# One SBUF pool for each weight tile and each weight pair, and last-stage pools laid on the ones that fall free first

## The chip, the cores and the metric

The kernel runs on one core of a Trainium2 chip. The metric is the device time of one execution in microseconds (us); the median of three executions is compared. A core has TensorE (PE; its weight loads are PEld), VectorE (DVE), ScalarE (ACT), GpSimd (POOL) and SyncE (SP), which here issues every transfer (DMA). Each engine works through its own queue strictly in order: an instruction that waits holds everything behind it on that engine.

## The reference, cut to what matters

Three blocks follow each other on 4 sequences of 576 tokens with 512 features: a linear attention, a mixer with a low-rank token part, and a second mixer. All in float32.

```python
def _moe_ref(x, U, V, w_ch1, w_ch2):            # w_ch1 512 x 2048, w_ch2 2048 x 512
    h = x.transpose(0, 2, 1) @ U @ V
    u = x + h.transpose(0, 2, 1)
    return u + np.maximum(u @ w_ch1, 0.0) @ w_ch2
def _moe2_ref(x, w_tok1, w_tok2, w_ch1, w_ch2): # w_ch1 512 x 1536, w_ch2 1536 x 512
    h = np.maximum(x.transpose(0, 2, 1) @ w_tok1, 0.0) @ w_tok2
    u = x + h.transpose(0, 2, 1)
    return u + np.maximum(u @ w_ch1, 0.0) @ w_ch2
```

## The kernel before, in words

Matmuls run on pairs of float32r tiles, a rounded high part and the rest, so each product is three matmuls (high-high, high-low, low-high). `split` makes such a pair: a copy on one engine, a subtraction on another. Weights arrive as 64-bit numbers. `load64` brings a block of 128x512 of them (512 KB) into a buffer `raw` by a transfer on SP, makes `w` and `r` from it by two ACT instructions (L140, L141), and puts them together by two DVE instructions (L143, L146). The second of these reads `raw` for the last time, and the buffer may then be filled again.

There are three stages. Stage A is the attention with part of the first mixer's channel work. Stage B takes each batch b in two halves of 288 tokens: `channel` runs the remaining 11 blocks of the first mixer's channel weights (tiles `wh`, `wl` of block f; blocks 0 to 6 in `wrB`). For each block TensorE computes `hp`, ACT makes `hhb` of it and DVE `hlb` (`relu_split`), and TensorE adds block f's part to `yb` one block later. After both halves `tokmix2` does the second mixer's token part: transposes `x2p`, their splits `x2h` and `x2l`, products `gp`, `gh` and `gl`, products `m2p`, an addition to `x2` (L607) and a store to DRAM (`u2D`).

Stage C, the last one, is the second mixer's channel part, over five chunks of tokens (464 wide, the last 448). The 12 blocks of weights are taken as six pairs. `pair_weights(p)` needs four loads: `raw_c{p}_0` and `_1` for the first-layer tiles `sh`, `sl` (seven combinations, four of them built in a scratch tile `st` on DVE and split by ACT and POOL), and `_2` and `_3` for the second-layer tiles `vh`, `vl`. For each chunk, `token_mats` builds seven combinations `th`, `tl` of the tokens `uc`; then `first(p)` forms products of 42 matmuls in PSUM tiles `xc`, `yc`, `zc`, `vc`, and `second(p)` adds 24 matmuls to the output. The weights of the six pairs are made once, while chunk 0 runs, and kept.

`raw` in stage C has two buffers. SBUF is filled from two sides. Each tile pool gets an address range when it is opened; a pool opened after others were closed is laid over their ranges, and a tile of it waits until the tiles below it have been used for the last time. The order on each engine is not written by hand: the framework's scheduler chooses it when it builds the program, from when it thinks that buffers fall free.

Of the kernel before, what the change touches and what calls it, by code (L numbers as in the profile page):

```python
# [8 lines left out]
F32 = mybir.dt.float32  # L9
F32R = mybir.dt.float32r  # L10
# [9 lines left out]
P = 128  # L20
# [5 lines left out]
C = 512  # L26
NPAIR = H // 2
NC = C // P
# [3 lines left out]
NF2 = 12  # L32
NA = 5
NR = NF2 - NA
EPS = 1e-06
CHUNKS = (464, 464, 464, 464, 448)
HM = 232
# [51 lines left out]
def body(ctx, tc, kq, vd, w_phi, U, V, wm1, wt1, wt2, wm2, out):  # L89
# [36 lines left out]
    wring = AB.enter_context(tc.tile_pool(name="wring", bufs=NA))  # L126
# [24 lines left out]
    def load_half(src, i, name, k, hi, lo):  # L151
        sl = slice(k * C, (k + 1) * C)
        w = load64(src[i][:, sl], P, C, f"{name}_{k}")
        split(w, hi[:, sl], lo[:, sl], WHI[name[0]][k], WLO[name[0]][k])

    def w_tiles(pool, name, slot=""):
        return [pool.tile([P, 2 * C], F32R, tag=f"{t}{slot}", name=f"{t}_{name}") for t in ("wh", "wl")]

    def load_w(pool, src, i, name, slot=""):
        hi, lo = w_tiles(pool, name, slot)  # L160
        for k in range(2):
            load_half(src, i, name, k, hi, lo)
        return hi, lo
# [374 lines left out]

    BX = ExitStack()
    with tc.using_default_side("right"):  # L540
        wrB = BX.enter_context(tc.tile_pool(name="wrB", bufs=1, reuse_waits="tile"))
        extra.append(BX.enter_context(tc.tile_pool(name="rawx", bufs=RAWX, reuse_waits="tile")))
        bc = BX.enter_context(tc.tile_pool(name="bc", bufs=1, reuse_waits="tile"))
        b2 = BX.enter_context(tc.tile_pool(name="b2", bufs=2, reuse_waits="tile"))
# [3 lines left out]
    psg = PB.enter_context(tc.tile_pool(name="psg", bufs=1, space=PSUM, reuse_waits="tile"))  # L548

    nB = NF1 - NA  # L550
    wB = [load_w(wrB, wm1, NA + f, f"b{f}", f) if f < NR else load_w(wring, wm1, NA + f, f"b{f}") for f in range(nB)]

    def channel(ws, uh, ul, res, o, nm, dst=None, pool=mlp):
        n = uh.shape[2]
# [65 lines left out]
    for t in range(NT):  # L620
        w = load64(wt1[:, t], P, 256, f"t1_{t}")
# [3 lines left out]
    for j in range(2):  # L625
        for k in range(2):
            sl = slice(k * N, (k + 1) * N)
            w = load64(wt2[:, j, sl], P, N, f"t2_{j}_{k}")
            split(w, T2H[:, j, sl], T2L[:, j, sl], "v", "v")

    for b in range(B):
        x2 = b2.tile([P, NC, S], F32, tag="x2", name=f"x2_{b}", bufs=1)
        for ch in range(2):
            nm = f"b{b}_{ch}"
            i = 2 * b + ch
            _, uh, ul = load_u(uD[i], nm) if i else u0
# [7 lines left out]
    PB.close()  # L644
    extra.clear()
    with tc.using_default_side("right"):
        wc = ctx.enter_context(tc.tile_pool(name="wc", bufs=1, reuse_waits="tile"))
    stc = ctx.enter_context(tc.tile_pool(name="stc", bufs=RAWB, reuse_waits="tile"))
    pc = ctx.enter_context(tc.tile_pool(name="pc", bufs=1, reuse_waits="tile"))
    psc = ctx.enter_context(tc.tile_pool(name="psc", bufs=1, space=PSUM, reuse_waits="tile"))  # L650

    def pair_weights(p):
        nm = f"c{p}"
        wa, wb = [load64(wm2[2 * p + i][:, :C], P, C, f"{nm}_{i}", stage=stc, wbufs=3) for i in range(2)]
        sh, sl = [wc.tile([P, 7, 256], F32R, tag=f"{t}{p}", name=f"{t}{p}") for t in ("sh", "sl")]
        split(wa.rearrange("p (a k) -> p a k", a=2), sh[:, 0:2], sl[:, 0:2], "a", "v")
        split(wb[:, 256:], sh[:, 2], sl[:, 2], "a", "v")

        def comb(i, a, b, op):
            t = stc.tile([P, 256], F32, tag="st", name=f"st{p}_{i}")  # L660
            nc.vector.tensor_tensor(out=t, in0=a, in1=b, op=op)
            split(t, sh[:, i], sl[:, i], "a", "p")
            return t

        s1 = comb(3, wb[:, :256], wb[:, 256:], ALU.add)
        s2 = comb(4, s1, wa[:, :256], ALU.subtract)
        comb(6, wa[:, 256:], s2, ALU.subtract)
        comb(5, wa[:, :256], wb[:, :256], ALU.subtract)
        vh, vl = [wc.tile([P, 2, C], F32R, tag=f"{t}{p}", name=f"{t}{p}") for t in ("vh", "vl")]
        for i in range(2):  # L670
            w = load64(wm2[2 * p + i][:, C:], P, C, f"{nm}_{2 + i}", stage=stc, wbufs=3)
            split(w, vh[:, i], vl[:, i], "a", "pv"[i])
        return sh, sl, vh, vl
# [3 lines left out]
    def token_mats(u, h, nm):  # L677
        b11, b12, b21, b22 = u[:, 0:2, :h], u[:, 0:2, h:], u[:, 2:4, :h], u[:, 2:4, h:]
        m = {}

        def put(i, src):
            th, tl = [pc.tile([P, 2, HM], F32R, tag=f"{t}{i}", name=f"{t}{i}{nm}")[:, :, :h] for t in ("th", "tl")]
            split(src, th, tl, "a", "v")
            m[i] = th, tl

        def comb(o, a, b):
            nc.vector.tensor_tensor(out=o, in0=a, in1=b, op=ALU.subtract)

        put(0, b11)
        t1 = pc.tile([P, 2, HM], F32, tag="tt", name=f"tt{nm}")[:, :, :h]  # L690
        comb(t1, b12, b11)
        put(2, b22)
        comb(b11, b22, t1)
        put(4, b11)
        put(3, t1)
        comb(b12, b22, b12)
        put(5, b12)
        put(1, b21)
        comb(b21, b21, b11)
        put(6, b21)  # L700
        return m

    def channel7(sl_, nm):
        n = sl_.stop - sl_.start
        h = n // 2
        u = pc.tile([P, NC, 2 * HM], F32, tag="u", name=f"u{nm}")[:, :, :n]
        nc.sync.dma_start(u, u2D[:, :, sl_])
        m = token_mats(u, h, nm)
        res = []
        for c in range(NC):  # L710
            res.append(pc.tile([P, 2 * HM], F32, tag="res", name=f"res{nm}_{c}", bufs=4)[:, :n])
            nc.sync.dma_start(res[c], u2D[:, c, sl_])
        yp = [psy.tile([P, 512], F32, tag=f"y{c}", name=f"y{nm}_{c}") for c in range(NC)]

        def product(o, w, wi, ti, start):
            wh, wl = w[0][:, wi], w[1][:, wi]
            th, tl = m[ti]
            for k in range(2):
                ks = slice(k * P, (k + 1) * P)
                g = [(wh[:, ks], th[:, k]), (wh[:, ks], tl[:, k]), (wl[:, ks], th[:, k])]  # L720
                for i, (l, r) in enumerate(g):
                    mm(o, l, r, start and k == 0 and i == 0, k == 1 and i == 2)

        def first(p):
            w = wC[p]
            pm = f"{nm}_{p}"
            X, Y, Z, V = [psc.tile([P, 512], F32, tag=t, name=f"{t}{pm}")[:, :h] for t in ("x", "y", "z", "v")]
            product(X, w, 0, 0, True)
            e = pc.tile([P, HM], F32, tag="e", name=f"e{pm}")[:, :h]
            cp("a", e, X)  # L730
            product(Y, w, 4, 4, True)
            product(Z, w, 3, 3, True)
            product(V, w, 5, 5, True)
            u2 = pc.tile([P, HM], F32, tag="u2", name=f"u2{pm}")[:, :h]
            nc.vector.tensor_add(u2, Y, e)
            hb = pc.tile([P, 2 * HM], F32, tag="hb", name=f"hb{pm}")[:, :n]
            nc.vector.tensor_add(hb[:, h:], V, u2)
            nc.vector.tensor_add(hb[:, h:], Z, hb[:, h:])
            product(X, w, 1, 1, False)
            product(V, w, 2, 6, False)  # L740
            product(Z, w, 6, 2, False)
            nc.vector.tensor_add(hb[:, :h], V, u2)
            ha = pc.tile([P, HM], F32, tag="ha", name=f"ha{pm}")[:, :h]
            nc.vector.tensor_add(ha, Z, u2)
            out2 = []
            for i in range(2):
                s = (2 * p + i) % 3
                out2.append([pc.tile([P, 2 * HM], F32R, tag=f"{t}{s}", name=f"{t}{pm}_{i}")[:, :n] for t in ("hh", "hl")])
            (ah, al), (bh, bl) = out2
            relu_split(X, ah[:, :h], al[:, :h])  # L750
            relu_split(ha, ah[:, h:], al[:, h:])
            relu_split(hb, bh, bl)
            return out2

        def second(p, hs):
            vh, vl = wC[p][2:]
            for i, (hh, hl) in enumerate(hs):
                for c in range(NC):
                    cs = slice(c * P, (c + 1) * P)
                    g = [(vh[:, i, cs], hh), (vh[:, i, cs], hl), (vl[:, i, cs], hh)]  # L760
                    for k, (l, r) in enumerate(g):
                        mm(yp[c][:, :n], l, r, p == 0 and i == 0 and k == 0, p == NF2 // 2 - 1 and i == 1 and k == 2)

        prev = None
        for p in range(NF2 // 2):
            hs = first(p)
            if prev is not None:
                second(*prev)
            prev = (p, hs)
        second(*prev)  # L770
        for c in range(NC):
            nc.vector.tensor_add(res[c], yp[c][:, :n], res[c])
            nc.sync.dma_start(out[:, c, sl_], res[c])

    t = 0
# [64 lines left out]
```

## Time and profile before

| what | value |
|---|---|
| median of three runs | 1117.73 us (1114.35 to 1120.58) |
| profiled execution: its own time | 1113.12 us |
| profiled execution: its span | 1111.3 us |
| TensorE matmuls | 1045.1 us busy, 94% |
| TensorE weight loads | 978.6 us, 88% |
| VectorE | 667.2 us, 60% |
| ScalarE | 458.5 us, 41% |
| GpSimd | 236.5 us, 21% |

Span is from the first to the last instruction; the own time also holds what lies around it. The shares are averages over stages of quite different kinds, so they say little about one place. Stage C begins at about 776 us of the span.

### The profile page before, as it was taken

The numbers are of one execution on the slowest core, as the hardware profiler recorded it, in microseconds if no ns is written. First come the engines' busy times: TensorE is split into PE (matmuls) and PEld (weight loads), VectorE is DVE, ScalarE is ACT, GpSimd is POOL, SyncE is SP. The second block draws the span as 40 slices with busy tenths as digits, with TensorE's granted clock in tenths as the row PEclk, the third lists the DMA queues.
The fourth block names the chain that finished last, engine by engine and source line by source line (L and its number), as shares of the span: only waits on it lengthen the run. The fifth ranks groups of instructions, "written<-read, shape, count | busy, mean of one in ns | idle before, by whom it ended". The sixth has DMA issues, their size and how long they took to land.

```text
span 1111.3 us, 18092 instructions
## 1 busy us (share of the span) xinstructions
PE 1045.1 (94%) x7068; PEld 978.6 (88%) x7068; DVE 667.2 (60%) x1221; ACT 458.5 (41%) x1079; POOL 236.5 (21%) x192
## 2 busy tenths in 40 slices
PE   9888999899899898999999999997687999999998
PEld 6777899799789698999999999996676899999998
DVE  7888997987995797523223214217788636363533
ACT  6776756665754675221111111115566313121211
POOL 3326655555643244000000000000233100000000
PEclk9998999999999798999999999999879999999999
DMA  6542322312211685102002101205433303020110
GB/s 208 173 133 62 117 70 73 97 56 79 81 55 38 216 284 169 42 22 86 22 9 80 42 1 44 81 1 172 136 123 133 103 1 104 1 94 9 37 33 34
DMA packets 62501, 92.18 MB, mean 83 GB/s; under 512 B 14672, under 2 KB 49232, under 8 KB 62416
## 3 DMA queue, kind: packets, MB, share of 16 engines
q1 hardware_dynamic: 62416, 91.03, 25.8%
q8 instruction: 55, 0.90, 0.3%
q14 instruction: 30, 0.25, 0.1%
HBM read 71.99 MB, written 18.95 MB: 82 GB/s over the span
## 4 chain that ended last, share of the span: by engine, by line
PE 69%; DVE 14%; DMA 7%; ACT 6%; issue 3%; POOL 1%; SPq 0%; DVEq 0%; ACTq 0%; POOLq 0%
PE yc L107 12%; PE hp_b L107 12%; PE yb L107 12%; PE hp_a L107 4%; PE yp L107 4%; PE pp L107 3%; PE vc L107 3%; PE xc L107 3%; PE zc L107 3%; PE kvp L107 3%; DMA raw_c<-in_wm_dram 3%; PE gp L107 2%; PE nm L107 2%; PE m2p L107 2%; PE dT L356 2%
## 5 line engine op out<-in xcount | busy, mean ns | idle before, releaser
L182 DVE SCALAR_TENSOR_TENSOR hlb<-hp_b,hhb 128x288 fp32r<-128x288 f32 x88 | 40.1, 456 | 185.2 <-ACT hhb L181 185.2
L181 ACT ACTIVATE hhb<-hp_b 128x288 fp32r<-128x288 f32 x88 | 36.1, 410 | 228.5 <-PE hp_b L107 225.8
L107 PE MATMUL hp_b<-uhb,wh_b 128*128 128x288 f32 x352 | 105.2, 300 | 3.4 <-DVE xT L493 3.4
L107 PE MATMUL hp_b<-ulb,wh_b 128*128 128x288 f32 x352 | 105.1, 299 | 0.0
L107 PE MATMUL hp_b<-uhb,wl_b 128*128 128x288 f32 x352 | 105.0, 299 | 0.0
L100 POOL TENSOR_TENSOR sl<-st,sh 128x256 fp32r<-128x256 f32 x24 | 22.6, 956 | 380.1 <-ACT sh L95 379.9
L107 PE MATMUL yb<-hlb,wh_b 128*128 128x288 f32 x352 | 97.3, 296 | 0.2
L107 PE MATMUL yb<-hhb,wl_b 128*128 128x288 f32 x352 | 97.1, 295 | 0.0
L107 PE MATMUL yc<-hlc,vh 128*128 128x464 f32 (+1 forms) x240 | 90.5, 377 | 0.0
L107 PE MATMUL yc<-hhc,vl 128*128 128x464 f32 (+1 forms) x240 | 90.4, 377 | 0.0
L107 PE MATMUL yc<-hhc,vh 128*128 128x464 f32 (+1 forms) x240 | 84.6, 382 | 2.4 <-ACT hhc L181 2.4
L100 POOL TENSOR_TENSOR qel<-qe,qeh 128x640 fp32r<-128x640 f32 (+1 forms) x48 | 71.7, 1505 | 26.2 <-ACT qeh L95 11.2
L107 PEld LDWEIGHTS hp_b<-uhb,wh_b 128*128 128x128 f32 x352 | 67.1, 191 | 4.9 <-DVE xT L493 3.7
L107 PE MATMUL yb<-hhb,wh_b 128*128 128x288 f32 x352 | 68.0, 296 | 0.0
L107 PEld LDWEIGHTS hp_b<-ulb,wh_b 128*128 128x128 f32 x352 | 67.4, 192 | 0.1
L107 PEld LDWEIGHTS hp_b<-uhb,wl_b 128*128 128x128 f32 x352 | 67.2, 191 | 0.0
L107 PEld LDWEIGHTS yb<-hlb,wh_b 128*128 128x128 f32 x352 | 66.1, 188 | 0.6 <-DVE hlb L182 0.6
L107 PEld LDWEIGHTS yb<-hhb,wl_b 128*128 128x128 f32 x352 | 66.3, 188 | 0.0
L100 POOL TENSOR_TENSOR kel<-ke,keh 128x512 fp32r<-128x512 f32 x36 | 48.6, 1362 | 62.5 <-ACT keh L95 61.0
L288 DVE TENSOR_REDUCE km<-pp 128x4 f32<-128x512 f32 x80 | 54.5, 682 | 12.3 <-PE pp L107 12.0
L100 DVE TENSOR_TENSOR kd<-pp,km 128x512 f32<-128x512 f32 x80 | 54.4, 681 | 0.7
L107 PEld LDWEIGHTS yb<-hhb,wh_b 128*128 128x128 f32 x352 | 53.9, 188 | 0.1
(249 smaller groups left out, 3209.1 us busy)
## 6 DMA issues: line engine op xcount, KB each, us to landing
raw_c<-in_wm_dram SPq DMA_DIRECT2D x24, 512.0 KB, 3.8
raw_b<-in_wm_dram SPq DMA_DIRECT2D x22, 512.0 KB, 4.6
kq<-in_kq_dram SPq DMA_DIRECT2D x80, 128.0 KB, 2.2
raw_a<-in_wm_dram SPq DMA_DIRECT2D x10, 512.0 KB, 4.4
rec<-rD SPq DMA_DIRECT2D x32, 144.0 KB, 2.9
uD<-xT SPq DMA_DIRECT2D x8, 576.0 KB, 3.5
sD<-xT SPq DMA_DIRECT2D x8, 576.0 KB, 5.4
x<-sD SPq DMA_DIRECT2D x8, 576.0 KB, 5.1
```

Of the source, the lines that this page charges most:

```text
L100: return ENG[e].tensor_tensor(out=o, in0=a, in1=b, op=ALU.subtract)
L107: nc.tensor.matmul(o, l, r, start=start, stop=stop, skip_group_check=True)
L181: nc.scalar.activation(hh, hp, AF.Relu)
L182: nc.vector.scalar_tensor_tensor(out=hl, in0=hp, scalar=0.0, in1=f32(hh), op0=ALU.max, op1=ALU.subtract)
L288: nc.vector.tensor_reduce(out=m, in_=pv, op=ALU.max, axis=AX.X, apply_absolute_value=True)
L356: nc.tensor.transpose(tp[:, o : o + r], ds["q", g, t][:r, j, :], ident[:r, :r])
```

## The change

The pool `wrB`, which held the tiles of seven blocks, becomes seven pools of one block each. The pool `wc`, which held the tiles of six pairs, becomes six pools of one pair each, all opened at the same point. Their tiles are made up front instead of inside `pair_weights`. The two scratch tiles `st` move from the small pool `stc` into the pool of pair 0, so that `stc` is now as large as the pool `stage` that it lies on. The tiles of `token_mats` and the tokens `uc` get a pool `pt` of their own. By the sizes, pair 0 with the scratch lies exactly on blocks 0 to 2, pair 1 on blocks 3 to 5, pair 2 on the rest of block 5, block 6 and the extra raw buffers. No arithmetic is added or taken away; the number of instructions on each compute engine and of bytes moved stays.

```diff
-        wrB = BX.enter_context(tc.tile_pool(name="wrB", bufs=1, reuse_waits="tile"))
+        wrB = [BX.enter_context(tc.tile_pool(name=f"wrB{f}", bufs=1, reuse_waits="tile")) for f in range(NR)]
...
-        wc = ctx.enter_context(tc.tile_pool(name="wc", bufs=1, reuse_waits="tile"))
+        wc = [ctx.enter_context(tc.tile_pool(name=f"wc{p}", bufs=1, reuse_waits="tile")) for p in range(NF2 // 2)]
     stc = ctx.enter_context(tc.tile_pool(name="stc", bufs=RAWB, reuse_waits="tile"))
+    pt = ctx.enter_context(tc.tile_pool(name="pt", bufs=1, reuse_waits="tile"))
     pc = ctx.enter_context(tc.tile_pool(name="pc", bufs=1, reuse_waits="tile"))
...
+    wcs = {}
+    for p in range(NF2 // 2):
+        w = wc[p]
+        wcs[p] = [w.tile([P, 7, 256], F32R, tag=f"{t}{p}", name=f"{t}{p}") for t in ("sh", "sl")]
+        wcs[p] += [w.tile([P, 2, C], F32R, tag=f"{t}{p}", name=f"{t}{p}") for t in ("vh", "vl")]
+        if p == 0:
+            sts = [w.tile([P, 256], F32, tag=f"st{i}", name=f"st{i}") for i in range(2)]
...
-        sh, sl = [wc.tile([P, 7, 256], F32R, tag=f"{t}{p}", name=f"{t}{p}") for t in ("sh", "sl")]
+        sh, sl, vh, vl = wcs[p]
...
-            t = stc.tile([P, 256], F32, tag="st", name=f"st{p}_{i}")
+            t = sts[i % 2]
...
-        u = pc.tile([P, NC, 2 * HM], F32, tag="u", name=f"u{nm}")[:, :, :n]
+        u = pt.tile([P, NC, 2 * HM], F32, tag="u", name=f"u{nm}")[:, :, :n]
```

The built program stands in the same order as before up to batch 0 of stage B, where five raw loads of stage C now go out on SP and three of them are turned into `w`. On TensorE the order is the same until the token part of the last batch (b3). The first place is the ACT queue in the second half of the last batch (names `hhb3_1_f`: batch 3, half 1, block f). Before, nothing stands between the blocks:

```order
L181 ACTIVATE hhb3_1_6_8865<-hp_b3_1_6_8852 128x288
L181 ACTIVATE hhb3_1_7_8894<-hp_b3_1_7_8881 128x288
L181 ACTIVATE hhb3_1_8_8923<-hp_b3_1_8_8910 128x288
L181 ACTIVATE hhb3_1_9_8952<-hp_b3_1_9_8939 128x288
L181 ACTIVATE hhb3_1_10_8981<-hp_b3_1_10_8968 128x288
L95 CAST x2h3_0_9020<-x2p3_0_9015 128x512
L95 CAST x2h3_1_9035<-x2p3_1_9030 128x512
L140 ACTIVATE w_c0_0_9185<-raw_c0_0_9183 128x512
```

With the change the same queue there reads so (`sh1` belongs to pair 1, `w_c1_2` to its third load):

```order
L181 ACTIVATE hhb3_1_6_8883<-hp_b3_1_6_8870 128x288
L140 ACTIVATE w_c1_1_9313<-raw_c1_1_9311 128x512
L141 ACTIVATE r_c1_1_9314<-raw_c1_1_9311 128x512
L95 CAST sh1_9231<-w_c1_0_9305 128x512
L140 ACTIVATE w_c1_2_9337<-raw_c1_2_9335 128x512
L141 ACTIVATE r_c1_2_9338<-raw_c1_2_9335 128x512
L181 ACTIVATE hhb3_1_7_8912<-hp_b3_1_7_8899 128x288
L95 CAST sh1_9231<-w_c1_1_9313 128x256
L95 CAST sh1_9231<-st1_9230 128x256
L95 CAST sh1_9231<-st0_9229 128x256
L181 ACTIVATE hhb3_1_8_8941<-hp_b3_1_8_8928 128x288
```

Weight work of pairs 0 to 2, which stood behind `x2h3_1`, now stands among the blocks from `hhb3_1_3` on. The second place follows at once, the ACT queue where the token part of batch 3 begins, with the change:

```order
L181 ACTIVATE hhb3_1_10_8999<-hp_b3_1_10_8986 128x288
L95 CAST sh2_9235<-w_c2_0_9357 128x512
L140 ACTIVATE w_c2_1_9365<-raw_c2_1_9363 128x512
L141 ACTIVATE r_c2_1_9366<-raw_c2_1_9363 128x512
L95 CAST x2h3_0_9038<-x2p3_0_9033 128x512
L140 ACTIVATE w_c2_2_9389<-raw_c2_2_9387 128x512
L141 ACTIVATE r_c2_2_9390<-raw_c2_2_9387 128x512
L95 CAST x2h3_1_9053<-x2p3_1_9048 128x512
```

Before, `x2h3_0` followed `hhb3_1_10` directly; now three instructions of pair 2 stand ahead of it and two ahead of `x2h3_1`. The third place is SP's queue around the stores of batch 3. Before, the order was this:

```order
L135 DMA raw_c1_0_9243<-in_wm2_dram 128x512
L707 DMA uc1_10138<-u2D_76 128x4x464
L608 DMA u2D_76<-x2_3_8344 512x1x288 x2
L135 DMA raw_c1_1_9251<-in_wm2_dram 128x512
L135 DMA raw_c1_2_9283<-in_wm2_dram 128x512
```

With the change it is this:

```order
L715 DMA uc1_10158<-u2D_76 128x4x464
L135 DMA raw_c3_2_9439<-in_wm2_dram 128x512
L608 DMA u2D_76<-x2_3_8362 512x1x288
L135 DMA raw_c3_3_9449<-in_wm2_dram 128x512
L608 DMA u2D_76<-x2_3_8362 512x1x288
L135 DMA raw_c4_0_9459<-in_wm2_dram 128x512
```

Ahead of the stores stand now 15 of the 24 weight loads in place of 5.

## Rows read from the trace of the kernel before

**Rows 1.** Page, busy tenths of TensorE in 40 equal slices of the span.

```profile
PE   9888999899899898999999999997687999999998
```

**Rows 2.** Stretches: length, busy us (instructions) by engine, TensorE's granted clock, DMA share, GB/s.

```profile
core 0: us, PE busy (x) PEld busy (x) DVE busy (x) ACT busy (x) POOL busy (x), PEclk, DMA share, GB/s
...
752.00:776.00 24.00, 19.32 (x109) 16.46 (x108) 18.88 (x37) 13.59 (x26) 1.42 (x2) 0.93 0.52 168
776.00:800.00 24.00, 17.04 (x94) 15.00 (x93) 17.82 (x34) 11.76 (x25) 7.48 (x7) 0.86 0.46 154
800.00:820.00 20.00, 15.17 (x65) 13.83 (x66) 16.04 (x29) 11.71 (x25) 5.53 (x6) 0.66 0.36 117
820.00:840.00 20.00, 15.08 (x90) 13.23 (x88) 15.12 (x29) 11.89 (x25) 4.49 (x5) 0.91 0.44 147
840.00:860.00 20.00, 15.07 (x85) 13.08 (x86) 17.50 (x35) 13.12 (x30) 7.73 (x6) 0.94 0.40 132
860.00:876.00 16.00, 15.25 (x105) 14.18 (x105) 12.52 (x24) 7.93 (x17) 4.01 (x4) 0.97 0.10 26
...
931.95:990.41 58.46, 58.46 (x398) 55.17 (x397) 28.23 (x63) 13.70 (x31) 0.00 (x0) 1.00 0.15 50
```

**Rows 3.** Timelines of ACT, DVE, TensorE: start, duration, instruction [idle before <-releaser].

```profile
752.57 0.59 ACT L95 CAST x2h<-x2p 128x512 fp32r<-128x512 f32 x1 [1.61 <-PE x2p L585]
...
766.10 1.27 DVE L182 SCALAR_TENSOR_TENSOR gl<-gp,gh 128x512 fp32r<-128x512 f32 x2
...
776.36 0.27 PE L107 MATMUL xc<-th0c,sh 128*128 128x232 f32 x1
...
780.93 0.56 PE L107 MATMUL xc<-th0c,sl 128*128 128x232 f32 x1 [3.97 <-DVE sl L100]
...
1107.29 0.37 PE L107 MATMUL yc<-hhc,vl 128*128 128x448 f32 x1
```

**Rows 4.** Chain that ended last, from 812 us: start, us, what.

```profile
812.78 3.78 DMA raw_c<-in_wm_dram
816.60 0.04 issue
816.65 0.67 ACT w_c L140
817.32 0.57 ACT r_c L141
...
819.21 0.61 DVE w_c L146
```

**Rows 5.** Timeline of SP's transfers, 690 to 880 us.

```profile
694.92 1.09 SPq L135 DMA_DIRECT2D raw_c<-in_wm_dram  x2
...
772.61 4.99 SPq L608 DMA_DIRECT2D u2D<-x  x2
785.61 70.96 SPq L135 DMA_DIRECT2D raw_c<-in_wm_dram  x19
```

**Rows 6.** Tile raw_c, transfers from issue to landing.

```profile
DMA to landing us min/median/max: 3.4/3.8/6.8
```

**Rows 7.** Timelines of TensorE, ACT and DVE in the last half-batch of stage B.

```profile
729.61 0.30 PE L107 MATMUL hp_b<-uhb,wh_b 128*128 128x288 f32 x1
...
747.37 0.41 ACT L181 ACTIVATE hhb<-hp_b 128x288 fp32r<-128x288 f32 x1 [2.77 <-PE hp_b L107]
...
747.81 0.46 DVE L182 SCALAR_TENSOR_TENSOR hlb<-hp_b,hhb 128x288 fp32r<-128x288 f32 x1 [2.73 <-ACT hhb L181]
```

**Rows 8.** Groups by shape, 776 to 876 us: busy us, mean ns, idle before.

```profile
L143 DVE SCALAR_TENSOR_TENSOR w_c<-w_c,r_c 128x512 int32<-128x512 int32 x21 | 15.9, 759 | 12.8 <-ACT w_c L140 6.8 <-ACT r_c L141 6.1
L146 DVE SCALAR_TENSOR_TENSOR w_c<-raw_c,w_c 128x512 int32<-128x512 int32 x21 | 15.5, 740 | 0.1
...
L100 POOL TENSOR_TENSOR sl<-st,sh 128x256 fp32r<-128x256 f32 x22 | 21.2, 976 | 51.2 <-ACT sh L95 51.1
...
L140 ACT ACTIVATE w_c<-raw_c 128x512 f32<-128x512 f32 x21 | 14.0, 670 | 10.9 <-DMA raw_c<-in_wm_dram 10.9
```

**Rows 9.** Line L661 on DVE: duration ns min/median/max, first and last start.

```profile
L661 DVE TENSOR_TENSOR st<-w_c,w_c x6: 411/426/1508, 781.6 to 862.3; 128x256 f32<-128x256 f32 x6
```

More of the change, by code (lines that the diff above doesn't have):

```diff
@@ L550, in body @@
     nB = NF1 - NA
-    wB = [load_w(wrB, wm1, NA + f, f"b{f}", f) if f < NR else load_w(wring, wm1, NA + f, f"b{f}") for f in range(nB)]
+    wB = [load_w(wrB[f], wm1, NA + f, f"b{f}", f) if f < NR else load_w(wring, wm1, NA + f, f"b{f}") for f in range(nB)]
     def channel(ws, uh, ul, res, o, nm, dst=None, pool=mlp):
@@ L668, in pair_weights @@
         comb(5, wa[:, :256], wb[:, :256], ALU.subtract)
-        vh, vl = [wc.tile([P, 2, C], F32R, tag=f"{t}{p}", name=f"{t}{p}") for t in ("vh", "vl")]
         for i in range(2):
@@ L681, in put @@
         def put(i, src):
-            th, tl = [pc.tile([P, 2, HM], F32R, tag=f"{t}{i}", name=f"{t}{i}{nm}")[:, :, :h] for t in ("th", "tl")]
+            th, tl = [pt.tile([P, 2, HM], F32R, tag=f"{t}{i}", name=f"{t}{i}{nm}")[:, :, :h] for t in ("th", "tl")]
             split(src, th, tl, "a", "v")
@@ L689, in token_mats @@
         put(0, b11)
-        t1 = pc.tile([P, 2, HM], F32, tag="tt", name=f"tt{nm}")[:, :, :h]
+        t1 = pt.tile([P, 2, HM], F32, tag="tt", name=f"tt{nm}")[:, :, :h]
         comb(t1, b12, b11)
```

## The prediction

> **What bounds the kernel now.** I read the slices of the page first. TensorE is at nine tenths or more nearly everywhere, and the longest hole is in slices 28 to 31 [rows 1], that is from about 750 to 860 us, where the last stage begins. The table by stretches shows its size [rows 2]: from 752 to 876 us TensorE is busy 96.9 of 124 us (the six rows added up), and in 800 to 820 its granted clock is 0.66, so part of what it does there runs at the lower of its two levels, 1.2 GHz. In the steady state a chunk of the last stage takes 58.46 us with TensorE busy all the time at clock 1.00 (the last row there). The first product of stage C stands at 776.36 and the last matmul ends at 1107.66 [rows 3], 331.3 us in all. Five chunks at 58.46, the last one a little shorter (448 of 464 columns), need about 291. So about **40 us are lost in stage C**, all of it in chunk 0: counted back from the end, chunk 0 ends at 1107.66 - 232.5 = 875.2, 98.8 us after its first product.
>
> What ends last in chunk 0 is read from the chain of waits: it runs through the weight loads, not through TensorE. One turn of a raw buffer [rows 4]: issue at 812.78, transfer 3.78, ACT 0.67 and 0.57, DVE's last read done at 819.82. That is 7.0 us a turn with two buffers, 3.5 a load at best. SP's timeline gives what is kept: 19 loads start within 70.6 us, 3.92 us a load [rows 5], 15.7 us for a pair of four, where TensorE needs 58.46/6 = 9.7 a pair. Weights bind, and the reason that they begin late is also on SP: only two loads go out early, at 694.92, and their ACT work stands behind the last batch's token part. The last load starts at 785.61 + 70.63 = 856.2, and chunk 0 ends 19.0 us after it.
>
> **The change part by part.** Nothing is removed or added in arithmetic; durations of instructions stay. What changes is when a tile's memory is free, and so the order.
>
> Early loads. Five loads go out in batch 0 and three of them become w, which puts six instructions of ACT (0.67 each, [rows 8]) and six of DVE (0.74 to 0.76) among blocks that leave ACT idle 2.77 us and DVE 2.73 us of each 3.19 [rows 7]. At most two of each stand between two blocks. Cost nothing; without that idle time 4 us. The loads that SP issues behind them wait for later events anyway.
>
> Pair work in the last half-batch. Pair 0 may be written when blocks 0 to 2 have been used for the last time, and block 2's part of yb ends at 729.61, where the next hp begins [rows 7]. From there I followed the queues by hand. ACT's five casts (2.3 us), POOL's subtraction, then w_c0_3 and its two DVE steps free the raw buffer at about 736, and load c1_1 goes out. ACT gets 1.2 to 3.3 us of weight work between two blocks, 2.2 in the mean, against 2.77 idle. A late hhb or hlb doesn't stop TensorE at once: block f's yb comes after another yb and another hp, 3.2 us after its hp ended, and ACT and DVE need about 1.0 of this, so 2.2 us of lateness are covered. Most at risk is hhb3_1_7, behind two loads (c1_1, c1_2) that go out at 736 and 738 and land at 740.5 and 742.3 [rows 6]: I get hlb about 0.6 us too late. Sum for the half-batch: **+1 us**, bounds 0 (all covered) and 4 (two more blocks held by a transfer of 5 rather than 3.8 us).
>
> A rule speaks against this part. DVE's L661 takes 0.41 us alone and up to 1.51 [rows 9], and the long ones stand beside POOL's subtractions, of 0.98 us [rows 8]. The Trainium skill (SBUF — State Buffer, Who interferes with whom) says that a VectorE instruction with two SBUF inputs and a GpSimd instruction that reads SBUF exclude each other for the whole instruction. The trace agrees. By the rule at its worst, five blocked instructions a pair at about 1 us would be 5 us a pair on DVE; by the rows the excess is some 1.4 us a pair (L143 and L146 0.06 to 0.08 above 0.68, and L661). Since hlb itself has one input in PSUM, I take the rows' value, which the 2.2 us of cover hold.
>
> Token part of batch 3. Here ACT's x2h3_0 now stands behind w_c2_1 and r_c2_1. Load c2_1 is four after c1_1, so out at 736 + 4 x 3.92 = 751.7, landed at 755.5, and ACT is done at 756.8, where before x2h3_0 began at 752.57 [rows 3]: +4. From there to the second gl DVE has 31 instructions where it had 23, eight more of 0.41 to 0.76, about 4.6 us, of which some 1.7 us fall into idle time that DVE had: +3. So gl comes at about 773.2 rather than 766.10 [rows 3]: **+7 us**, bounds +2 (transfers land early, the cover holds) and +12 (each of three transfers held to 5.5 us). On TensorE 24 products of pair 0 (2.7 us) now stand between the two halves of m2p, where the additions of the first half were waited for.
>
> Start of chunk 0. With gl 7 us late, the first half of m2p ends at 776.5, then 2.7 us of products, then the second half with four more products, ending at 782.9. By then 28 matmuls of chunk 0 are done, 3.1 us. Chunk 0 has in effect begun at 779.8, 3.4 us later than the 776.36 of before, but pairs 0 and 1 are complete and pair 2 nearly.
>
> Weights for the rest of chunk 0. Eighteen loads after c1_1 at 3.92 us put the last one at 806.6. SP's queue holds c4_0 behind the second store of x2, which waits for the last addition, at about 784.5, where the rate alone gives 736 + 11 x 3.92 = 779.1; so 5.4 later, **812**, in place of 856.2. With the 19.0 us that follow, weights would allow the end of chunk 0 at 831. TensorE at full rate ends it at 779.8 + 58.5 = 838.3. So TensorE binds, narrowly. DVE is close behind it: in 800 to 860 it was busy 48.7 of 60 us [rows 2], and it now does the same in about 50. I therefore put **5 us of stalls** on chunk 0, bounds 0 (weights always 7 us ahead) and 20 (half of the 40 of before stays).
>
> The sum: chunk 0 ends at 838.3 + 5 = 843.3 in place of 875.2, **32 us** earlier; what follows is unchanged. Against the profiled execution's own 1113.1 this gives 1081; that execution is 4.6 below the median of the runs, so against the median of 1117.7 I forecast **1086 us**. The half-batch's 1 us is within the 7 (the transposes begin that much later).
>
> **The rivals.**
> 1. The stream of weights stays the bound. For it: the turn of 7.0 us goes through ACT and DVE, and in the last half-batch each step now stands behind a block that comes every 3.2 us. Against: ACT and DVE are then idle for 85% of the time. It decides from 4.6 us a load (last load later than 843.3 - 19.0 = 824.3). At 5.5 the last load goes out at 736 + 18 x 5.5 + 5.4 = 840, chunk 0 ends at 859, gain 16, 1102 us.
> 2. Slower than before: transfers ahead of hhb, x2h and gh. Eight loads (c1_1 to c3_0) are waited for on ACT in front of work that TensorE needs. If each holds TensorE for more than 4.0 us, all 32 us are gone; at 5, 1126 us. For it: the order rows show these waits. Against: landing takes 3.8 in the median and 6.8 at most [rows 6], and each is issued before ACT arrives; even 3.0 more each makes 24 us.
> 3. The change does little: a tile of pair 0 or 1 waits for memory used until the token part, so that its work starts as late as before, behind a queue that is no shorter. 1118 us. The sizes of the ranges speak against it.
> 4. The token part isn't delayed and chunk 0 has no stall: 5 + 5 more, gain 42, 1076 us. DVE's load speaks against it.
>
> **How the numbers follow.** Forecast (gain 24 to 38) 0.60, rival 1 (gain 8 to 24) 0.20, rival 4 0.12, rival 3 0.05, rival 2 0.03. About 0.5%, 5.6 us here, is what a measurement of this kernel can tell from no change. Faster 0.92, same 0.05, slower 0.03. Lowest by the bounds: no stall, token part +2 and half-batch 0 give 32 + 5 + 5 + 1 = 43, 1075. Highest: 20 us of stalls and 3 more in the half-batch give 32 - 18 = 14, 1104. The range 1075 to 1104 holds the forecast, most of rival 4 and two thirds of rival 1, about 0.82.
>
> **What would show it.** Right: sh0 casts at about 730 in the last half-batch, the first raw_c load of the second group at 736, blocks still 3.2 us apart, gl at about 773, the last raw_c load at about 812, TensorE at clock 1.00 from 776 on, and the second chunk's steady state reached some 32 us earlier. Wrong: hp or yb more than 5 us apart after 730 (rival 2), a last load after 825 with TensorE waiting for sl or sh (rival 1), or sh0 still at about 770 (rival 3).

## The result, and the profile after

The changed kernel takes 1087.65 us (median of 4 runs, 1085.81 to 1089.89), the kernel before 1119.1 us in the same set (4 runs, 1114.35 to 1120.58). The ratio is **0.9727, 95% interval 0.969 to 0.9764**: 2.7% faster. The forecast was 1086. The profiled execution took 1085.81 us, its span is 1084.0; for it the forecast was 1081.

The page's slices of TensorE after the change, which answer to [rows 1]: the hole in slices 28 to 31 is down to two slices, 29 and 30, between eight and nine tenths.

```profile
PE   8888999899989898999999999999889999999998
```

The table by stretches (length, busy us by engine, granted clock of TensorE, DMA share, GB/s) answers to [rows 2]. From 820 us on TensorE is busy all the time at clock 1.00; what is still lost lies in the token part of batch 3 and in the first 40 us of chunk 0. The row to remember is that of 768 to 776, where the clock is 0.52.

```profile
730.00:752.00 22.00, 21.24 (x156) 20.55 (x156) 17.58 (x27) 14.15 (x33) 9.55 (x10) 1.00 0.31 96
752.00:760.00 8.00, 6.19 (x36) 4.83 (x36) 6.21 (x12) 4.32 (x9) 0.00 (x0) 1.00 0.75 222
760.00:768.00 8.00, 5.09 (x24) 3.53 (x24) 7.34 (x14) 6.04 (x14) 3.92 (x2) 1.00 0.77 280
768.00:776.00 8.00, 6.86 (x18) 4.97 (x19) 8.00 (x15) 5.55 (x11) 5.03 (x4) 0.52 0.13 23
776.00:784.00 8.00, 8.00 (x58) 8.00 (x57) 6.37 (x15) 2.83 (x5) 0.00 (x0) 0.84 0.91 302
784.00:792.00 8.00, 7.27 (x59) 6.99 (x58) 7.92 (x17) 5.32 (x14) 3.45 (x4) 1.00 0.50 155
792.00:800.00 8.00, 6.28 (x39) 5.64 (x38) 5.87 (x10) 3.07 (x6) 1.97 (x2) 1.00 0.48 147
800.00:820.00 20.00, 18.32 (x123) 16.45 (x123) 18.29 (x35) 12.61 (x28) 5.01 (x5) 1.00 0.38 120
820.00:840.00 20.00, 20.00 (x131) 18.68 (x130) 16.59 (x33) 10.38 (x24) 4.95 (x5) 1.00 0.09 27
840.00:860.00 20.00, 20.00 (x139) 18.91 (x138) 11.37 (x26) 4.53 (x11) 0.00 (x0) 1.00 0.43 144
```

SP's timeline answers to [rows 5]: the second group of loads begins at 735.66, and eight loads are left at 790.33, where 19 were left at 785.61.

```profile
735.66 18.72 SPq L135 DMA_DIRECT2D raw_c<-in_wm_dram  x6
...
759.43 0.33 SPq L135 DMA_DIRECT2D raw_c<-in_wm_dram  x1
...
762.76 11.61 SPq L135 DMA_DIRECT2D raw_c<-in_wm_dram  x2
...
777.56 0.33 SPq L135 DMA_DIRECT2D raw_c<-in_wm_dram  x1
780.72 0.56 SPq L608 DMA_DIRECT2D u2D<-x  x1
782.28 0.33 SPq L135 DMA_DIRECT2D raw_c<-in_wm_dram  x1
786.36 0.56 SPq L608 DMA_DIRECT2D u2D<-x  x1
790.33 29.61 SPq L135 DMA_DIRECT2D raw_c<-in_wm_dram  x8
```

Timelines of ACT, DVE and TensorE, in this order, with the places of [rows 3, 7]: pair 0 is written at 729.49, as soon as block 2 has been used; hhb3_1_7 stands behind an awaited transfer; the first gl and the first product of chunk 0 are late; the last matmul ends 27.3 us earlier than before.

```profile
729.49 0.93 ACT L95 CAST sh<-w_c 128x512 fp32r<-128x512 f32 x2 [1.18 <-PE yb L107]
...
742.56 0.68 ACT L140 ACTIVATE w_c<-raw_c 128x512 f32<-128x512 f32 x1 [1.40 <-DMA raw_c<-in_wm_dram]
743.15 0.66 ACT L141 ACTIVATE r_c<-raw_c 128x512 int32<-128x512 uint32 x1
743.71 0.39 ACT L181 ACTIVATE hhb<-hp_b 128x288 fp32r<-128x288 f32 x1
...
756.55 0.56 ACT L95 CAST x2h<-x2p 128x512 fp32r<-128x512 f32 x1
...
768.40 0.68 DVE L100 TENSOR_TENSOR x2l<-x2p,x2h 128x512 fp32r<-128x512 f32 x1
...
773.90 0.68 DVE L182 SCALAR_TENSOR_TENSOR gl<-gp,gh 128x512 fp32r<-128x512 f32 x1
...
789.59 0.68 DVE L146 SCALAR_TENSOR_TENSOR w_c<-raw_c,w_c 128x512 int32<-128x512 int32 x1
...
753.16 0.60 PE L585 MATMUL x2p<-ident,x 128*128 128x128 f32 x4
...
769.14 0.80 PE L107 MATMUL gp<-x2l,T1H 128*128 128x512 f32 x1 [3.35 <-DVE x2l L100]
769.73 0.63 PE L107 MATMUL gp<-x2h,T1L 128*128 128x512 f32 x1
...
774.88 0.44 PE L107 MATMUL m2p<-T2L,gh 128*128 128x288 f32 x1
...
779.34 0.27 PE L107 MATMUL xc<-th0c,sh 128*128 128x232 f32 x1
...
1079.96 0.37 PE L107 MATMUL yc<-hhc,vl 128*128 128x448 f32 x1
```

The chain of waits (start, us, what) shows what made that x2l late: a GpSimd subtraction, then a VectorE instruction on `st`, with x2l right behind it at 768.40. After them come the last products gp and the first half of m2p, 10.36 us.

```profile
764.08 2.91 POOL sl L100
767.01 1.47 DVE st L670
...
769.14 4.93 PE gp L107 x10
774.07 5.43 PE m2p L107 x24
```

### The profile page after: what moved, and what is told of

The parts are those of the page before. It is cut to its first block, busy times and chain, and to the rows that moved or that the text cites. A ratio compares the mean times of both kernels' runs of the same rounds, so it can differ in the third digit from the quotient of the medians.

```text
span 1084.0 us, 18092 instructions
## 1 busy us (share of the span) xinstructions
PE 1034.0 (95%) x7068; PEld 968.7 (89%) x7068; DVE 670.1 (62%) x1221; ACT 457.7 (42%) x1079; POOL 239.5 (22%) x192
## 4 chain that ended last, share of the span: by engine, by line
PE 72%; DVE 12%; DMA 5%; issue 4%; ACT 4%; POOL 1%; SPq 0%; DVEq 0%; POOLq 0%; ACTq 0%
PE yc L107 15%; PE hp_b L107 12%; PE yb L107 11%; PE hp_a L107 4%; PE yp L107 3%; PE zc L107 3%; PE xc L107 3%; PE vc L107 3%; PE pp L107 3%; PE kvp L107 3%; PE gp L107 2%; PE m2p L107 2%; PE nm L107 2%; PE dT L356 2%; DMA raw_c<-in_wm_dram 1%
## 5 line engine op out<-in xcount | busy, mean ns | idle before, releaser
L107 PE MATMUL hp_b<-uhb,wh_b 128*128 128x288 f32 x352 | 105.1, 300 | 3.4 <-DVE xT L493 3.4
L107 PE MATMUL hp_b<-ulb,wh_b 128*128 128x288 f32 x352 | 105.1, 299 | 0.0
L107 PE MATMUL hp_b<-uhb,wl_b 128*128 128x288 f32 x352 | 105.0, 299 | 0.0
L107 PE MATMUL yb<-hlb,wh_b 128*128 128x288 f32 x352 | 97.6, 297 | 0.7 <-DVE hlb L182 0.4
L107 PE MATMUL yb<-hhb,wl_b 128*128 128x288 f32 x352 | 97.1, 295 | 0.0
L107 PE MATMUL yc<-hlc,vh 128*128 128x464 f32 (+1 forms) x240 | 89.2, 372 | 1.9 <-DVE hlc L182 1.9
L107 PE MATMUL yc<-hhc,vl 128*128 128x464 f32 (+1 forms) x240 | 89.2, 372 | 0.0
L107 PE MATMUL yc<-hhc,vh 128*128 128x464 f32 (+1 forms) x240 | 83.2, 373 | 0.3 <-ACT hhc L181 0.3
L100 POOL TENSOR_TENSOR vl<-w_c,vh 128x512 fp32r<-128x512 f32 x6 | 8.2, 1364 | 292.8 <-PE hp_b L107 288.9
L107 PEld LDWEIGHTS hp_b<-uhb,wh_b 128*128 128x128 f32 x352 | 67.1, 191 | 4.9 <-DVE xT L493 3.6
L107 PE MATMUL yb<-hhb,wh_b 128*128 128x288 f32 x352 | 68.1, 296 | 0.3 <-ACT hhb L181 0.3
L107 PEld LDWEIGHTS yb<-hlb,wh_b 128*128 128x128 f32 x352 | 66.1, 188 | 1.9 <-DVE hlb L182 1.9
L107 PEld LDWEIGHTS hp_b<-ulb,wh_b 128*128 128x128 f32 x352 | 67.4, 191 | 0.1
L107 PEld LDWEIGHTS hp_b<-uhb,wl_b 128*128 128x128 f32 x352 | 67.2, 191 | 0.0
L107 PEld LDWEIGHTS yb<-hhb,wl_b 128*128 128x128 f32 x352 | 66.2, 188 | 0.0
L107 PEld LDWEIGHTS yb<-hhb,wh_b 128*128 128x128 f32 x352 | 53.9, 188 | 0.7 <-ACT hhb L181 0.6
```

The costliest lines, as they stand in the source:

```text
L100: return ENG[e].tensor_tensor(out=o, in0=a, in1=b, op=ALU.subtract)
L107: nc.tensor.matmul(o, l, r, start=start, stop=stop, skip_group_check=True)
```

## The experiments

Each kernel is the changed one with an edit. All were timed against the kernel before on the same chip (its medians there 1117.0 to 1117.6 us); a ratio is to it.

**The four parts of the change, each undone by itself.** The order on the engines is again the scheduler's.

One pool for the tiles of blocks 0 to 6:

```diff
-        wrB = [BX.enter_context(tc.tile_pool(name=f"wrB{f}", ...)) for f in range(NR)]
+        wrB = BX.enter_context(tc.tile_pool(name="wrB", ...))
```

> The changed kernel with the weight tiles of stage B back in one pool. Pair 0 then gets its place when the seventh block of the last half-batch has been used, about 12 us later than 729.5, so 19 of 24 loads start near 741 instead of 735.7. Theory A (the gain is the earlier start of the weights' stream, which in the changed kernel has some 9 us of slack: last load 819.6 plus 19.0 us of work behind a last load, against an end of chunk 0 at 847.8): last load near 831, chunk 0 ends near 850, and the token part of batch 3, with less pair work in it, ends up to 7 us earlier: 1084 to 1096 us, best guess 1091. Theory B (the stream still sets the end, load by load): 12 us lost in full, 1100 us. Theory C (the gain does not come from stage B's pools): 1088 us with the same order of stalls.

Measured: **1093.7 us**, ratio 0.9799 (0.9769 to 0.983). One pool for the six pairs:

```diff
-        wc = [ctx.enter_context(tc.tile_pool(name=f"wc{p}", ...)) for p in range(NF2 // 2)]
+        wc = ctx.enter_context(tc.tile_pool(name="wc", ...))
```

> The changed kernel with the six pairs in one pool: five loads still stand ahead of batch 1, but all pair work waits behind the last gh of batch 3. Theory A (the stream's start decides): 19 loads start near 772 to 780 as in the kernel before (785.6), the last lands near 850, chunk 0 ends near 869: 1108 to 1118 us, best guess 1112. Theory C (the early five loads alone bring it): 1090 us. The token part should be as in the kernel before (first gl near 766), since no pair work stands in it.

Measured: **1117.03 us**, 1.0006 (0.9988 to 1.0024). The token tiles of chunk 0 back in `pc`:

```diff
-    pt = ctx.enter_context(tc.tile_pool(name="pt", ...))
...
-        u = pt.tile([P, NC, 2 * HM], F32, tag="u", name=f"u{nm}")[:, :, :n]
+        u = pc.tile([P, NC, 2 * HM], F32, tag="u", name=f"u{nm}")[:, :, :n]
```

> The changed kernel with the tiles of the last stage's tokens back in the pool of its other tiles; the order on TensorE and ScalarE is that of the changed kernel but for two rows. Theory A: nothing, 1088 us within 0.4%. Theory C (the place of the token tiles, free when stage B's tokens are done, brings part of it): chunk 0's token tiles wait for the weight ring of stage B, 1 to 6 us slower, 1089 to 1094 us.

Measured: **1089.1 us**, 0.9757 (0.9727 to 0.9787). The scratch back in `stc`:

```diff
-            t = sts[i % 2]
+            t = stc.tile([P, 256], F32, tag="st", name=f"st{p}_{i}")
```

> The changed kernel with the scratch st back beside the staging tiles, whose pool then reaches over the token tiles of stage B by 2 KB. Theory A: all pair work stands behind batch 3's tokens again, as before the change, with 19 loads from about 782: 1108 to 1119 us, best guess 1114; the separate pools are then worth next to nothing by themselves. Theory C (each part of the change brings its share): about halfway, 1095 to 1105 us.

Measured: **1112.75 us**, 0.9951 (0.9931 to 0.9972). So the gain isn't a sum of parts. The pair pools and the 2 KB of scratch are each needed for nearly all of it, since either one, undone, puts the pair work into or behind batch 3's token part again: the first sh cast stands at 767.85 and at 759.92 in place of 729.49. With the pairs in one pool the five early loads still go out (at 453.57) and gain nothing by themselves; with the scratch in `stc` they are gone too, and two loads go out at 694.25 as before the change. The block pools are worth 4 to 6 us by the medians (two sets of the changed kernel; against the second the intervals overlap a little), the pool `pt` nothing that can be measured. The trace with the blocks in one pool, which has no pair work among blocks 3 to 7, starts chunk 0 earlier than the changed kernel (775.11 against 779.34) and ends it later; the early stream pays for the late start.

**Does the stream of weights still bind?**

```diff
-    wC = [pair_weights(p) for p in range(NF2 // 2)]
+    wC = [pair_weights(p) for p in range(NF2 // 4)] * 2
```

> The changed kernel with the weights of pairs 3 to 5 left out: these pairs use those of pairs 0 to 2 again, so 12 of 24 loads and their ScalarE, VectorE and GpSimd work are gone. Theory A (in the changed kernel TensorE's own work sets the end of chunk 0; only the stalls between 785 and 820, some 4 us, hang on the weights' work): 1080 to 1086 us, best guess 1084. Theory B (the weights' stream still sets the end): all of chunk 0's surplus goes, 1070 us or less.

Measured: **1081.87 us**, 0.9676 (0.9662 to 0.9691), 5.8 below the changed kernel (7.9 below its second set, further down, which ran on the same chip). From the first transposes to the last matmul it is 7.3 us shorter, 1.0 of it ahead of the first product. So 6.3 us of chunk 0 hang on the weights of pairs 3 to 5; theory B is out.

**What the token part of batch 3 costs.** `tok` keeps the two instructions that make x2h and x2l of each tile of tokens; the hold uses the last. (`split` now returns them, so the kernels that hold have other line numbers: their L105 is L107 here.)

```diff
-    wC = [pair_weights(p) for p in range(NF2 // 2)]
+    wC = [pair_weights(p) for p in range(2)]
+    with tc.issue_after(tok[B - 1, NT - 1][0].ins), tc.issue_after(tok[B - 1, NT - 1][1].ins):
+        wC += [pair_weights(p) for p in range(2, NF2 // 2)]
```

> The changed kernel with the ScalarE and VectorE work of pairs 2 to 5 held behind the last x2h and x2l of batch 3. Theory A (the pair work in the token part costs the some 7 us that were forecast for it, and the stream has slack to pay for the delay): first gl near 767 instead of 773.9, first xc near 773 to 775 instead of 779.3, last load near 823, chunk 0 ends 843 to 847 instead of 847.8: 1082 to 1088 us, best guess 1084. Theory D (the held work is missing in chunk 0, the stream binds as it does with stage B's weights in one pool): 1089 to 1094 us.

Measured: **1082.41 us**, 0.968 (0.9666 to 0.9695): faster than the changed kernel, by a little more than was expected. Its first product of chunk 0 stands at 773.45 and its last load at 824.2, near what was worked out; the first gl came at 770.50 rather than 767, of which 2.6 us are a later start of the whole last half-batch. Two variants were to tell ScalarE's and VectorE's part apart. The first holds the token tiles of the last stage too:

```diff
+        with tc.issue_after(tok[B - 1, NT - 1][1].ins):
             m = token_mats(u, h, nm)
```

> As the run that holds pairs 2 to 5, and the VectorE work on the token tiles of the last stage's chunks held behind the last x2l of batch 3 as well. Theory A: first gl near 766, first xc near 773, but seven pairs of token tiles come later on VectorE: 1081 to 1088 us, best guess 1083. Theory D: 1089 to 1094 us.

Measured: **1086.65 us**, 0.9716 (0.9694 to 0.9738). The second has this last edit alone:

> The changed kernel with the VectorE work on the token tiles of chunk 0 alone held behind the last x2l of batch 3; the pair work stays where it is. If VectorE's queue (the x2l that TensorE awaits 3.35 us at 769.1) is the dear part of the token part: first gl near 770.5 and the end 2 to 3 us earlier, 1085 us (1082 to 1088). If ScalarE's casts behind awaited transfers are: gl near 773 and no change, 1088 us.

Measured: **1091.68 us**, 0.9768 (0.9753 to 0.9782). Both missed their best guess, the second its whole forecast. In the second TensorE waits 1.19 us for the x2l for which it waited 3.35:

```profile
770.37 0.50 PE L105 MATMUL gp<-x2l,T1H 128*128 128x512 f32 x1 [1.19 <-DVE x2l L99]
```

Yet the token part is only 1.2 us shorter (19.56 us against 20.74), where the hold of pairs 2 to 5 makes it 5.9 shorter. So most of the delay hangs on the pair work and not on VectorE's token tiles; how it divides between ScalarE and VectorE stays open. The work that was held falls into chunk 0, where VectorE has no room. Of that last run the stretch and the timeline of TensorE show it: in 776 to 800 VectorE is busy 23.00 of 24 us, and TensorE waits for its hlc, hac and u2c.

```profile
776.00:800.00 24.00, 19.58 (x141) 18.11 (x142) 23.00 (x46) 11.83 (x26) 5.87 (x6) 1.00 0.55 177
```

```profile
790.93 0.37 PE L105 MATMUL xc<-th0c,sh 128*128 128x232 f32 x1 [1.37 <-DVE hlc L180]
...
792.67 0.37 PE L105 MATMUL zc<-th3c,sh 128*128 128x232 f32 x1 [0.81 <-DVE hac L753]
...
796.62 0.37 PE L105 MATMUL yc<-th4c,sh 128*128 128x232 f32 x1 [1.89 <-DVE u2c L744]
```

**Does more come out of the stream, and how much may be held?** Batch 3's stores are taken off SP's queue, in the kernel that holds pairs 2 to 5:

```diff
-            nc.sync.dma_start(u2D[...], x2[:, :, sl])
+            (nc.gpsimd if b == B - 1 else nc.sync).dma_start(u2D[...], x2[:, :, sl])
```

> The kernel that holds pairs 2 to 5 behind batch 3's tokens (1082.4 us), with batch 3's two u2D stores issued on GpSimd's queue, so that the weight loads on SyncE's queue don't stand behind them. If the stream has an end to gain (in that kernel TensorE still waits 0.4 to 0.8 us seven times between 797 and 830, for work on freshly loaded weights): the last load 3 to 4 us earlier than 824.5 and 1 to 3 us off the end, 1080 to 1081 us. If those stalls are VectorE's own queue: 1082 to 1083 us, same. If the stores make GpSimd's subtractions late: 1084 us or more.

Measured: **1084.47 us**, 0.9707 (0.968 to 0.9733). The same with `nc.scalar`:

> As the run with batch 3's u2D stores on GpSimd's queue, but on ScalarE's. The weights' stream gains the same; ScalarE then waits for VectorE's sums ahead of two casts: 1080 to 1083 us, and 1084 or more if that delays hhc or ec on TensorE's path.

Measured: **1083.53 us**, 0.969 (0.9661 to 0.9718). Neither can be told from 1082.41. On SP nothing stands between the loads any more, and yet 13 of them take 51.94 us, 4.3 each. The last 14 loads start between 768.65 and 823.8, where they started between 770.09 and 824.2 with the stores on SP. So the stores on SP's queue don't set the rate. Between 765 and 826 us of the trace with GpSimd's stores SP's queue waits 14 times, 60.6 us in all, for DVE's second step (L146 in the changed kernel), which frees a raw buffer: what sets the rate is the turn of the two buffers through ACT and DVE. The seven waits of TensorE that the first expectation puts down to fresh weights are mostly others: of the six that the trace with pairs 2 to 5 held shows between 797 and 830, one is for sh and five are for hhc, ec and hac, chunk 0's own work.

```profile
772.20 51.94 SPq L133 DMA_DIRECT2D raw_c<-in_wm_dram  x13
```

Pair 1 held as well (`range(1)` and `range(1, NF2 // 2)` in the edit above):

> The changed kernel with pairs 1 to 5 (not only 2 to 5) held behind the last x2h and x2l of batch 3, so that only pair 0 is worked on early. 15 loads instead of 11 then stand behind batch 3's u2D stores. Theory A (the end is the later of TensorE's own work and the last load plus some 20 us): last load near 840, the end of chunk 0 near 860: 1096 to 1102 us, best guess 1099. Theory C (a load is cheap to delay, as the hold of pair 2 showed): 1081 to 1086 us. The last half-batch should end about 1 us earlier than with pair 1's work in it.

Measured: **1096.86 us**, 0.9822 (0.9795 to 0.985), as theory A has it. Last, the changed kernel again beside these three:

> The changed kernel itself once more beside these, unaltered: 1086 to 1090 us by its first runs.

Measured: **1089.77 us**, 0.9749 (0.9722 to 0.9776). Against this the hold of pairs 2 to 5 is 0.7% faster, with intervals apart; against the first set, 0.5%, with intervals that touch.

One table over all traces with all 24 loads. "uhb" is the start of the cast uhb of the last half-batch, "half" is from there to the first x2p, "tokens" from there to the first gl; the last load is the start of the last raw_c on SP (a group's start and length, less 0.33), and the end of chunk 0 is the end of the last matmul less the 232.5 us of the prediction. All in us.

| kernel | uhb | half | tokens | last load | end of chunk 0 | end behind last load |
|---|---|---|---|---|---|---|
| before | 715.8 | 36.2 | 14.2 | 856.2 | 875.2 | 19.0 |
| scratch in stc | 715.1 | 36.2 | 14.6 | 853.3 | 872.3 | 19.0 |
| pairs in one pool | 717.5 | 36.2 | 13.4 | 855.7 | 880.2 | 24.5 |
| pairs 1 to 5 held | 717.1 | 36.2 | 14.7 | 839.4 | 858.8 | 19.4 |
| blocks in one pool | 714.7 | 36.2 | 19.5 | 830.5 | 852.0 | 21.5 |
| both held | 720.1 | 37.1 | 13.8 | 830.0 | 850.4 | 20.3 |
| stores on ACT | 721.1 | 37.0 | 15.0 | 829.2 | 848.7 | 19.5 |
| pairs 2 to 5 held | 718.0 | 37.7 | 14.8 | 824.2 | 844.4 | 20.2 |
| stores on POOL | 717.2 | 37.0 | 14.8 | 823.8 | 844.9 | 21.1 |
| **changed** | 715.4 | 37.7 | 20.7 | 819.6 | 847.8 | 28.2 |
| changed, again | 721.9 | 37.0 | 22.2 | 826.4 | 854.6 | 28.2 |
| token tiles in pc | 718.2 | 37.6 | 20.9 | 821.6 | 849.9 | 28.2 |
| token tiles held | 718.0 | 38.0 | 19.6 | 822.5 | 853.9 | 31.4 |

The traces reach uhb at 714.7 to 721.9 us, a spread that arises ahead of it, so loads and ends of different traces are compared from there. Then the two traces of the changed kernel agree (last load 104.2 and 104.5 us after uhb, end of chunk 0 132.4 and 132.7), and with pairs 2 to 5 held chunk 0 ends at 126.4, 6.0 us earlier; the medians differ by 5.2 and 7.4.

The traces fall into two kinds. In eight of the first nine chunk 0 ends 19 to 21.5 us behind the last load: weights bind. (The other one, with 24.5, has TensorE's granted clock at 0.58 in 860 to 870, behind its last load.) In the last four it ends 28 us or more behind it: the stream has slack, and what binds is the late start and VectorE.

## Why the prediction came out nearly right

Its frame held: the changed kernel gains by an earlier stream of weights until TensorE's own work binds, and pays part of it in batch 3's token part. On the profile the gain in chunk 0 is 875.2 - 847.8 = 27.4 us where 32 were forecast. That the median came so near to 1086 is in part luck. The forecast adds the 4.6 us by which the profiled execution of before lay under its median; that of the changed kernel lies 1.8 under its own. By the profiled executions the gain is 27.3 us, by the medians 31.5, by those of the second set of the changed kernel 27.3 (1117.04 - 1089.77). By its steps:

- **Early loads, 0 us.** From the cast uhb that stands ahead of the early loads (413.63, before 414.01) to that of the last half-batch (715.43, before 715.75) it takes 301.8 us, before 301.7. Right.
- **Pair work in the last half-batch, +1 us.** The half took 37.7 in place of 36.2, +1.5, inside the bounds of 0 and 4. It is pair 1's: with only pair 0 there (pairs 1 to 5 held) it takes 36.2. hhb3_1_7 stands behind an awaited transfer, as worked out. TensorE waits 0.7 us in this half, for one hhb and one hlb.
- **Token part, first gl +7 at 773.2.** It came at 773.90, +7.8; x2h3_0 at 756.55 where 756.8 was worked out. Holding pairs 2 to 5 takes 5.9 us out of the token part (20.7 to 14.8), so it is the work of pair 2, as said, and of the first load of pair 3. From x2h3_0 to the first gl it took 3.8 more where 3 were forecast. But that near hit holds an error that cancels: from the first gp behind the late x2l to the first m2p it takes 4.86 us (769.14 to 774.00), with pairs 2 to 5 held 3.00, so some 1.9 us of the 7.8 are the lower clock of the next step, which the prediction didn't count. The queues alone gave some 6.
- **The first half of m2p ending at 776.5, "then 2.7 us of products".** This is the term that was mis-sized. The products of chunk 0 behind the half did take 2.7 us (779.34 to 782.01). But the half ended at 779.5, and its 24 products took 5.43 us (the chain above); the prediction counted products at full clock throughout. TensorE had been busy 11.28 of the 16 us from 752 to 768 and had just waited 3.35 us for x2l, and in 768 to 776 its granted clock is 0.52: most of the stretch is at 1.2 GHz. Products of gp and m2p show 0.63 and 0.44 us there. In the kernel that holds pairs 2 to 5, where the clock stays at 1.00, they show 0.40 and 0.29:

```profile
766.65 0.40 PE L105 MATMUL gp<-x2l,T1H 128*128 128x512 f32 x1
...
769.45 0.29 PE L105 MATMUL m2p<-T2H,gh 128*128 128x288 f32 x1
```

  The second half of m2p ended at about 785.7 (the next product starts at 785.65) instead of 782.9. By the prediction's own count chunk 0 began in effect at 785.7 - 3.1 = 782.6, **2.8 later** than the 779.8 forecast: some 0.7 by gl, the rest by the clock. The sign "clock 1.00 from 776 on" failed with it: 0.84 in 776 to 784. That the end of chunk 0 would move by the full 2.8 is not shown; no run changes the clock alone.
- **5 us of stalls in chunk 0.** By the same sum 847.8 - 782.6 - 58.5 = 6.7; the run without the weights of pairs 3 to 5 gives 6.3. With the 2.8 this 1.7 more makes, as a sum, the 4.5 by which the gain fell short.
- **Last load at 812.** It went out at 819.6: the eight loads from c4_0 on began 5.8 later, and ran at 29.28/7 = 4.18 us each rather than 3.92, 1.8 more. What held c4_0 last was not the second store of x2, which went out at 786.36, but the raw buffer: DVE's second step on c3_2 began only at 789.59 and ended as c4_0 went out at 790.33. That wait is not in the prediction's sum. It cost nothing here, since 28.2 us are left behind it. "TensorE binds, narrowly" is right.
- **The rule on VectorE and GpSimd.** The groups by shape, 728 to 860 us, give the price on VectorE:

```profile
L143 DVE SCALAR_TENSOR_TENSOR w_c<-w_c,r_c 128x512 int32<-128x512 int32 x21 | 17.0, 809 | 10.1 <-ACT r_c L141 7.9 <-ACT w_c L140 2.1
L146 DVE SCALAR_TENSOR_TENSOR w_c<-raw_c,w_c 128x512 int32<-128x512 int32 x21 | 16.1, 769 | 0.1
L670 DVE TENSOR_TENSOR st<-w_c,w_c 128x256 f32<-128x256 f32 x6 | 5.2, 862 | 0.6 <-POOL sl L100 0.6
L670 DVE TENSOR_TENSOR st<-w_c,st 128x256 f32<-128x256 f32 x6 | 5.1, 848 | 0.0
```

  Above 0.68 and 0.41 us these are 2.7 + 1.9 + 2.7 + 2.6 = 9.9 us, some 1.8 a pair, near the 1.4 taken and far from 5. What was left out is the other side: in the dense token part two of GpSimd's subtractions took 2.90 and 2.94 us where 0.976 is usual [rows 8], and x2l stood behind one of them. The Trainium skill (SBUF — State Buffer, Who interferes with whom) says that the one that issues first holds the shared pair for its whole instruction and the other blocks, whichever it is; the trace agrees, as far as GpSimd's spans, which are rough, can tell: VectorE's `st` that started at 767.01, 0.07 us behind a GpSimd subtraction, took 1.47 us where 0.41 is usual. That this and not the sheer number of instructions made x2l late was only argued; the hold takes both away.

The rivals: the first (the stream stays the bound) did not come. Its point of decision, a last load later than 824.3, is 108.5 us after the uhb of before (715.75). The table puts it near that, somewhat earlier: counted from uhb, the weights bind in the traces with a last load at 106.2 or later, and have slack in those with one at 104.5 or earlier. In absolute times the rule fails for the second trace of the changed kernel (826.4, with slack). The fourth (no token delay, 1076) is what holding pair 2 aims at; it gave 1082, with the slack of the stream used up (20.2 us behind the last load). The second shows in TensorE's 0.7 us of waits in the half-batch and 1.8 for x2h in the token part, far from the 4.0 a load that it needed; the third found no trace. Two sums of the prediction don't follow from its parts: rival 4 takes off 5 us for a token part put at 7, and the upper end of the range leaves out that part's bound of +12. Neither touches the forecast.

## What to carry to other kernels

When loads are let out early, count two ends: the last load plus the work behind it, and TensorE's own work from the late start. Then hold back early work where it stands ahead of a short serial part, until the first end comes up to the second; here holding pairs 2 to 5 gave 0.5 to 0.7% more, and holding pair 1 too lost it again. In a memory plan look for the one tile that makes a pool reach over memory still in use: 2 KB of scratch decided over some 25 us.

## What the runs showed of the hardware

A wait can cost more than its own length. TensorE was busy 11.28 of the 16 us from 752 to 768, and the 3.35 us in which it then waited for x2l were followed by about 9 us at its lower clock, 1.2 GHz (769 to 778; granted 0.52 in 768 to 776), in which ten gp and some twenty m2p products took 0.2 and 0.1 us more each by their starts, about 4 us. With pairs 2 to 5 held it was busy 14.06 of the 16 us from 752 to 768, waited 1.31 us for the same x2l, and its clock stayed at 1.00. Before the change two waits of 2.12 and 2.34 us in the token part were followed by some 3 us of m2p products at 0.44 us, beginning here:

```profile
771.54 0.40 PE L107 MATMUL m2p<-T2H,gh 128*128 128x288 f32 x1 [2.34 <-DVE x L607]
...
772.24 0.44 PE L107 MATMUL m2p<-T2L,gh 128*128 128x288 f32 x1
```

So not all of the 4 us is a price of the change. What the 0.66 in 800 to 820 [rows 2] cost before can't be told from these runs, since the weights bound there.
